# Forgetting attention with a SwiGLU block behind it: the stored order of batch 0's start is replaced

## The chip, the cores and the metric

The kernel runs on one core of a Trainium2 chip. The metric is the device time of one execution in microseconds, as a median over runs. Five engines work side by side and keep to their own order of instructions: TensorE (PE in the profile; its weight loads are PEld), VectorE (DVE), ScalarE (ACT), GpSimd (POOL) and SyncE (SP). SP, ACT and POOL also start DMA transfers.

## The reference

Everything is given and returned in float32; the kernel multiplies in bfloat16.

```
B, H, S, D = 8, 8, 576, 64
scores = q @ k.T / sqrt(D);  cum = cumsum(log(clip(f, 1e-4, 1)))
scores = where(causal, scores + cum[i] - cum[j], -1e9)
attn = softmax(scores) ;  x = attn @ v         # heads side by side: 4608 tokens x 512
xn = x / sqrt(mean(x*x) + 1e-6) * rms_g
out = (silu(xn @ w_gate) * (xn @ w_val)) @ w_out     # 512 -> 1536 -> 512
```

## The kernel before

The work is cut into some 1,550 pieces, each a few instructions of one engine. `ORDER`, a text of names, says in which order the pieces are emitted; every engine then runs its own pieces in that order, and a piece that must wait holds up all later pieces of its engine. Nothing else sets the order. `name@A`, `@D`, `@O` or `@S` puts a piece on ACT, DVE, POOL or SP in place of its default engine. `name*n` has `warm_up` (L249) issue idle matmuls on a tile of zeros, n blocks of 128 columns, in front of the piece; they compute nothing that is used, and only keep TensorE occupied.

The names that matter below, for batch b, pair of heads p, block of 128 tokens j:

- `Lq Lk Lv Lqk`: loads of q, k, v and of the tails (tokens 512 to 575) into ten staging buffers `st`. Batch 0 loads q and k in quarters of four heads by 256 tokens (`load_half`, L463); `Lq0.0` and `Lk0.0` are heads 0 to 3, tokens 0 to 255. `lf`: the load of f (L271, on ACT). `rg`: the 2 KB of rms_g (L352, on POOL). `wg0..2`, `wv0..2`, `wo0..1`: weights, cast on the way (L381, L393, on POOL).
- `Cq Ck Cqk`: the cast of a staged load to bf16 (L222). `Sv`: v times the decay (L451).
- `tr0.hp`: PE transposes of q and k of one pair (L540; `tr1.p`, `tr2.p` for batches 1 and 2, L528); `keeptr...q` and `.k`: their copies out of PSUM (L222). `trt`, `keeptrt`: the same for the tails (L558).
- `clip log scan expo twice turn_dec keep_dec`: the decay, from f to the factors that `Sv` needs. `fetch_ln`, `fetch`: the activation tables of Ln and Exp.
- `turn_rg keep_rgT spread_rg keep_rg`: rms_g turned and spread over the partitions (L357, L360, L366, L222).
- `far`: a mask written into the scores' PSUM bank (L664); `sc`: scores (L679); `esc`: their exp on ACT (L688); `msc`: a mask on POOL (L694). `sc4`, `exp4`, `mask4`: the tail's diagonal.
- `val`: probabilities times v (L714); `xpo`: the division, into X (L721, L722). `sq rs xn`: the norm (L729, L735, L739). `xtr kxtr`: the turned activations of batches 0 and 1 (L766, L222).
- `g v th ga hga`: gate and value products of a group of tokens, and the SwiGLU (L863, L868, L872, L879). `pj o so`: the last product, its copy and its store (L889, L222, L897). Groups 0 and 1 hold 256 tokens each, the others 512.

Batch 0 is worked in two parts: `HEAD`, tokens 0 to 255 (score banks named `.0`), so that group 0 can start early, and `REST` (banks `.512`, `.1024`, `.384`). The scores have two PSUM buffers (`sc`), the products of many kinds share three (`ff`), and one more (`po`) is for `val`. From `g0.0` on the attention of the next batches is laced between the products of the groups. TensorE's order before has 51 pieces ahead of `g0.0` and 64 from there to `g2.0`.

Of the kernel before, what the change touches and what calls it, by code (L numbers as in the profile page):

```python
# [14 lines left out]
B, H, S, D = 8, 8, 576, 64  # L15
# [7 lines left out]
one lf far Lq1.0 Lq0.0 Lq0.1@A ident Lk0.0 Lv0.1@A tri identb clear Lk0.1 Lq0.3@A fetch_ln rg Lk0.2 clip Lk0.3@A log Cq0.1@A scan Lq0.2 Cq0.0@A Lqk01  # L23
fetch Lv0.0 Ck0.0 tr0.01*72 Lqk11@A far0.1.0 keeptr0.01.q tr0.00 keeptr0.01.k far0.3.0 expo keeptr0.00.q sc0.1.0 Ck0.1@D Cq0.3@A twice keeptr0.00.k@D
tr0.02 Lv0.40 turn_dec esc0.1.0 Lk1.0 tr0.03 turn_rg Ck0.2@O Lqk00@A far0.0.0 keeptr0.03.q keep_rgT keeptr0.03.k sc0.0.0 Lqk10@A Ck0.3 sc0.3.0
keeptr0.02.k tr0.12 esc0.3.0 keep_dec Lq1.3 Cq0.2 keeptr0.02.q Sv0.1@O Lv0.2@A tr0.10*2 keeptr0.12.q far0.1.1024 esc0.0.0 keeptr0.12.k@D spread_rg
Cq1.0 Lv0.3 keeptr0.10.k Cqk0@D far0.2.0 keeptr0.10.q sc0.2.0 Lk1.3@A Sv0.0@O trt0 esc0.2.0 Lv0.41 keeptrt0 wv0 sc0.1.1024*6 Cqk1@A val0.0.0 Lk1.2
val0.4.0:ff keep_rg val0.6.0:ff xpo0.0.0 k4.0 Lk1.1 esc0.1.1024 val0.2.0:ff sc0.0.384 Lq1.2 wg0 xpo0.2.0 esc0.1.384 Lq1.1 sc4.0 xpo0.4.0 wg1 exp4.0
xpo0.6.0 esc0.3.384 far0.3.1024*4 esc0.0.384 Ck1.0 esc0.2.384 sc0.3.1024 Sv0.2 sq0.0 sc0.1.512 Lv1.41 trt1 esc0.3.1024 keeptrt1 Lv1.40 Sv0.3@O
esc0.1.512 Lqk20 sc0.0.512*9 Sv0.4 Lqk21 sq0.1 far0.0.1024*2 wv1 sc0.0.1024 esc0.0.512 rs0.0 Lk2.0 esc0.0.1024 sc0.2.512*6 tr1.0 mask4.0 xn0.1  # L30
far0.2.1024 keeptr1.0.q@A k4.1 Lv1.0 sc0.2.1024 esc0.2.512 keeptr1.0.k@D val0.0.2 val0.1.2:ff xpo0.0.2 esc0.2.1024 sc0.3.512 Cq1.2@O xpo0.1.2 val0.2.2
xn0.0 Ck1.1 esc0.3.512 val0.5.2:ff val0.3.2:ff xpo0.5.2 xtr0.0 wg2 sc1.0.512 Cq1.1@A kxtr0.0 xpo0.3.2 esc1.0.512 xtr0.1 Cq1.3 val0.4.2:ff xpo0.2.2
val0.6.2:ff wv2 Lq2.0 xpo0.4.2 kxtr0.1 val0.7.2 xpo0.6.2 Ck1.3@O tr1.1 esc1.0.0 xpo0.7.2 sc4.1 Ck1.2 g0.0 Lv1.3 keeptr1.1.k@D sq0.2 keeptr1.1.q v0.0f
th0.0 sq0.3 ga0.0 g0.2 exp4.1 sq0.4 hga0.0 sc1.0.1024 th0.2 rs0.2 tr1.3 esc1.1.512 ga0.2 xn0.2 v0.2f*4 keeptr1.3.q@A keeptr1.3.k@D esc1.0.1024 g0.4
hga0.2 xtr0.2 xn0.3 th0.4 tr1.2 kxtr0.2@A sc1.1.0 ga0.4 keeptr1.2.k xtr0.3 v0.4f esc1.1.1024 Lq2.3 kxtr0.3@D keeptr1.2.q g1.0 esc1.1.0 hga0.4 Lv1.1
v1.0f th1.0 msc1.1.1024 Lv1.2@A ga1.0 sc1.2.512 Lq3.3 esc1.2.512 g0.6 mask4.1 hga1.0 xn0.4 g1.2 Ck2.0 th0.6 ga0.6 v1.2f Sv1.4 th1.2 esc1.2.0 Lk2.1
ga1.2 g1.4 Cqk2@A hga1.2 xtr0.4 sc1.2.1024 th1.4 v0.6f kxtr0.4@A Lk2.3 Sv1.0@O ga1.4 esc1.2.1024 Lq2.1 g0.8 hga0.6 wo0 v1.4f th0.8 Cq2.0 esc1.3.512
ga0.8 v0.8f msc1.0.1024 Lqk31 hga1.4 g1.6 hga0.8 Lk3.0 msc1.2.1024 trt2 Sv1.2@D th1.6 sc1.3.0 keeptrt2@A wo1 v1.6f esc1.3.0 ga1.6 Lq3.2 Sv1.3 g1.8
hga1.6 Lqk30 tr2.0 th1.8 Sv1.1@D g0.10 keeptr2.0.k ga1.8 k4.2@A val1.4.0 keeptr2.0.q Cq2.3@A v1.8f th0.10 xpo1.4.0 val1.2.0:ff esc1.3.1024 ga0.10
val1.0.0 hga1.8 v0.10f Cq3.3@A msc1.3.1024 xpo1.0.0 Cq2.1@A tq3.3 g1.10 Ck2.1@A hga0.10 Ck2.3 xpo1.2.0 sc2.0.512 th1.10 val1.5.0 ga1.10 val1.3.0:ff  # L40
esc2.0.512 v1.10f xpo1.3.0 xpo1.5.0 val1.6.0:ff sc4.2 val1.1.0:ff xpo1.6.0 val1.7.0 xpo1.1.0 pj0.0.0 xpo1.7.0 hga1.10 sq1.1 sq1.0 tr2.1 exp4.2
pj0.0.0e sq1.3 keeptr2.1.q pj0.1.0 sq1.4 keeptr2.1.k@D Lk2.2 sq1.2 o0.0.0@D Lk3.3 Lq2.2@A rs1.0 pj0.1.0e esc2.0.0 pj1.0.0 Cqk3 xn1.1 Lv2.3@A tt3
o0.1.0 xn1.4 Lv2.0@A so0.1.0 pj1.0.0e Cq3.2@D sc2.0.1024 o1.0.0 xn1.2 xtr1.1 esc2.1.512 pj1.1.0 xn1.3 esc2.0.1024 xn1.0 kxtr1.1@D Lv2.1 Ck3.0@A
msc2.0.1024 xtr1.2 Ck2.2@A pj1.1.0e kxtr1.2 Lq3.0 tr2.3 o1.1.0 xtr1.3 tq3.2 Cq2.2 keeptr2.3.k sc2.1.0 kxtr1.3@D keeptr2.3.q@A Sv2.3 xtr1.0 tr2.2
Lv2.41@A kxtr1.0 Lk3.1 xtr1.4 keeptr2.2.q g2.0 keeptr2.2.k mask4.2 Lv2.40@A kxtr1.4 v2.0f Lq4.0 th2.0 esc2.1.1024 g2.1 ga2.0 Lq3.1 esc2.1.0 hga2.0
v2.1f tk3.0 g2.2 th2.1 Ck3.3@A ga2.1 sc2.2.512 th2.2 Sv2.4 hga2.1 v2.2f Lv2.2@A ga2.2 esc2.2.512 g2.3 hga2.2 Sv2.0 v2.3f th2.3 Lv6.40 Ck3.1@A ga2.3
msc2.1.1024 g2.4 Lv3.3 k4.3@A Lk3.2 hga2.3 esc2.2.0 v2.4f Sv2.1@D Lv3.40 g2.5 th2.4 Sv2.2 tk3.1 ga2.4 sc2.2.1024 th2.5 v2.5f esc2.2.1024 Lq4.1 ga2.5
hga2.4 Lk4.0 val2.0.0 esc2.3.512 msc2.2.1024 g2.6 hga2.5 tk3.3 Cq4.0@A Cq3.0@D v2.6f th2.6 Cq3.1@A ga2.6 sc2.3.0 Ck3.2@A tq3.1 xpo2.0.0 g2.7 esc2.3.0
hga2.6 v2.7f th2.7 tq3.0 esc2.3.1024 val2.4.0 ga2.7 val2.1.0:ff xpo2.4.0 g2.8 msc2.3.1024 Lv3.1 xpo2.1.0 val2.3.0 tk3.2 hga2.7 th2.8 Sv3.3 v2.8f ga2.8
val2.5.0:ff Lv3.41 xpo2.3.0 sc4.3 val2.7.0:ff Lqk41 xpo2.5.0 exp4.3 val2.2.0 mask4.3 so1.0.0@S hga2.8 sc3.0.512 xpo2.2.0 Lq4.3 esc3.0.512 g2.9 Sv3.1  # L50
xpo2.7.0 Lv3.2 val2.6.0 th2.9 Lv3.0 Ck4.0 v2.9f esc3.0.0 ga2.9 Sv3.4 Lk4.1 g2.10 xpo2.6.0 hga2.9 tk4.0 sc3.0.1024 th2.10 so0.0.0 v2.10f esc3.0.1024
ga2.10 g2.11 esc3.1.512 hga2.10 msc3.0.1024 v2.11f sq2.1 Sv3.2 th2.11 pj2.0.0 sq2.4 ga2.11 Lqk40 Cq4.1 sq2.2 Lk4.3 hga2.11 sq2.3 Lq4.2 sq2.0 pj2.0.0e
tq4.0 sc3.1.0 rs2.0 pj2.1.0 esc3.1.1024 esc3.1.0 xn2.0 xn2.4 tx2.0.3 msc3.1.1024 pj2.1.0e xn2.2 sc3.2.512 esc3.2.512 Lv4.2 pj2.2.0 Sv3.0 Lv4.3 o2.1.0
xn2.1 tx2.2.3 esc3.2.0 so2.1.0 o2.0.0 sc3.2.1024 so1.1.0 tx2.1.3 Cq4.2@A val3.0.0 Cq4.3@D esc3.2.1024 pj2.2.0e xpo3.0.0 pj2.3.0 tq4.3 esc3.3.512
msc3.2.1024 xn2.3 Ck4.3@D pj2.3.0e val3.1.0 Ck4.1@D tk4.3 o2.3.0 val3.3.0:ff xpo3.1.0 o2.2.0 val3.2.0:ff xpo3.3.0 sc3.3.0 tq4.1 xpo3.2.0 g3.0 Lk4.2
val3.5.0 th3.0 v3.0f Lv4.40 xpo3.5.0 esc3.3.0 Lv4.1 ga3.0 g3.1 esc3.3.1024 Cqk4@D Lk5.0 v3.1f hga3.0 th3.1 Lv4.41 msc3.3.1024 g3.2 ga3.1 tq4.2
val3.4.0 hga3.1 th3.2 val3.7.0:ff tk4.1 xpo3.4.0 v3.2f ga3.2 val3.6.0 xpo3.7.0 Lk6.2 g3.3 xpo3.6.0 Lq5.0 v3.3f hga3.2 tt4 th3.3 sq3.4 ga3.3 g3.4 sq3.2
hga3.3 v3.4f th3.4 Ck5.0@D sq3.1 ga3.4 g3.5 Lk5.1 Lq5.3 hga3.4 sc4.0.512 th3.5 Ck6.2 tk5.0 v3.5f Ck4.2@A ga3.5 Sv4.4 esc4.0.512 g3.6 hga3.5 tx2.3.4
# [907 lines left out]
```

## Time and profile before

| | |
|---|---|
| median of 5 runs | 381.34 us (380.26 to 382.61) |
| the profiled execution | 384.89 us, span 383.1 us |
| mean granted TensorE clock | 0.987 |
| PE busy | 367.3 us (96%) |
| DVE, ACT, POOL busy | 260.1, 220.4, 136.1 us |
| `g0.0`, first product of group 0, starts at | 37.29 us |
| `pj0.0.0`, first last-product, starts at | 69.11 us |
| `g2.0` starts at | 83.59 us |
| DMA moved | 52.58 MB |

Busy time is what an engine spent on instructions; an idle matmul counts as busy too. The row of the granted clock says how much of TensorE's full rate was granted in each slice. A row of a timeline gives start, length, engine, line, operation, and in brackets how long the engine stood idle ahead of it and what ended that. A DMA row gives the time from issue to landing. The times of `g0.0`, `pj0.0.0` and `g2.0` are read in PE's timeline, from the rows of L863 and L889 in their order.

### The profile page before, as it was taken

Reading aid. Unit: us, or ns where it says so; the run is one execution under the profiler, and the core shown is the slowest. Engines: PE = TensorE matmul, PEld = TensorE weight load, DVE = VectorE, ACT = ScalarE, POOL = GpSimd, SP = SyncE. Lnnn points to the kernel's source line nnn. Section 1 sums busy time; section 2 is a strip of 40 time slices with the busy share of each in tenths; the row PEclk is TensorE's granted clock in tenths of the full one; section 3 lists DMA queues with packets and bytes.
Section 4 is the critical chain, followed back from the end, with each engine's and each line's share of the span. In section 5 each row is a group of like instructions: output and inputs, shape, how many; then the busy total and the mean of one; then the engine's idle time right before and its main releaser. Section 6 shows DMA issues by size and latency. Waiting matters only on the chain.

```text
span 383.1 us, 8139 instructions
## 1 busy us (share of the span) xinstructions
PE 367.3 (96%) x3103; PEld 196.2 (51%) x3144; DVE 260.1 (68%) x497; ACT 220.4 (58%) x369; POOL 136.1 (36%) x249
## 2 busy tenths in 40 slices
PE   7779999999999999999899999999999999999996
PEld 3547788554644544445454544454445544444443
DVE  5547888678866778768757765778467876763560
ACT  5578978578697477354755587346565422322312
POOL 3556193236468145533431564020830111000001
PEclk9869999999999999999999999999999999999999
DMA  9999999597699889999959794641300234002002
GB/s 216 238 255 218 211 212 214 121 230 148 127 225 182 174 161 176 184 182 165 185 135 183 149 197 111 153 85 41 76 36 8 64 82 124 3 0 82 29 0 110
DMA packets 144774, 52.58 MB, mean 137 GB/s; under 512 B 128188, under 2 KB 141120, under 8 KB 144736
## 3 DMA queue, kind: packets, MB, share of 16 engines
q1 hardware_dynamic: 126992, 37.64, 50.8%
q0 software_dynamic: 6016, 8.79, 10.8%
q10 hardware_dynamic: 11728, 5.65, 6.1%
q8 instruction: 24, 0.39, 0.5%
q14 instruction: 14, 0.11, 0.1%
HBM read 37.90 MB, written 9.44 MB: 124 GB/s over the span
## 4 chain that ended last, share of the span: by engine, by line
PE 67%; DMA 10%; issue 6%; DVE 6%; ACT 5%; POOL 3%; SPq 1%; POOLq 0%; ACTq 0%; DVEq 0%
PE ff L863 41%; PE ff L889 16%; DMA st<-in_q_dram 5%; PE sc L679 4%; PE po L714 3%; DMA QK<-ld 3%; DVE xn L739 2%; ACT PT L688 2%; POOL PT L694 1%; ACT th L868 1%; DMA st<-in_k_dram 1%; DMA out_dram<-ores 1%; DVE X L722 1%; PE ff L714 1%; DVE hT L879 1%
## 5 line engine op out<-in xcount | busy, mean ns | idle before, releaser
L868 ACT ACTIVATE th<-ff 128x512 f32<-128x512 f32 x108 | 64.5, 597 | 91.4 <-PE ff L863 86.7
L863 PE MATMUL ff<-xT,wv 128*128 128x512 bf16 (+1 forms) x466 | 109.7, 357 | 1.1 <-DVE ga L872 0.4
L863 PE MATMUL ff<-xT,wg 128*128 128x512 bf16 (+1 forms) x464 | 109.3, 357 | 1.2 <-DVE X L722 0.2
L688 ACT ACTIVATE PT<-sc 128x1024 bf16<-128x1024 f32 (+2 forms) x100 | 96.2, 991 | 16.4 <-PE sc L679 14.3
L872 DVE SCALAR_TENSOR_TENSOR ga<-th,ff 128x512 f32<-128x512 f32 x108 | 74.0, 685 | 41.7 <-ACT th L868 41.2
L889 PE MATMUL ff<-wo,hT 128*128 128x512 bf16 (+1 forms) x433 | 97.4, 373 | 0.8 <-issue 0.2
L879 DVE SCALAR_TENSOR_TENSOR hT<-ga,ff 128x512 bf16<-128x512 f32 x108 | 73.7, 684 | 15.2 <-PE ff L863 6.5
L694 POOL TENSOR_SCALAR_AFFINE_SELECT PT<-PT 128x256 bf16<-128x256 bf16 (+1 forms) x84 | 43.1, 537 | 74.2 <-ACT PT L688 74.0
L863 PEld LDWEIGHTS <-wg 128*128 128x128 bf16 x480 | 45.2, 98 | 44.4 <-issue 2.1
L863 PEld LDWEIGHTS <-wv 128*128 128x128 bf16 x480 | 44.6, 98 | 43.5 <-issue 3.3
L889 PEld LDWEIGHTS <-hT 128*128 128x128 bf16 x444 | 42.4, 98 | 47.7 <-issue 1.4
L714 PEld LDWEIGHTS <-PT 128*128 128x128 bf16 x896 | 33.7, 98 | 11.8 <-issue 3.2
L739 DVE SCALAR_TENSOR_TENSOR xn<-X,rs,rgb 128x512 bf16<-128x512 f32 x40 | 32.8, 845 | 8.9 <-POOL rs L735 8.8
L897 POOL DMA_DIRECT2D out_dram<-ores x16 | 9.2, 578 | 68.2 <-ACT ores L222 36.0
L222 ACT COPY ores<-ff 128x512 f32<-128x512 f32 (+1 forms) x25 | 14.2, 569 | 33.2 <-PE ff L889 27.6
L222 POOL CAST ld<-st 128x512 bf16<-128x512 f32 x34 | 21.1, 628 | 30.6 <-DMA st<-in_q_dram 11.5
L679 PE MATMUL sc<-QK 64*128 64x256 bf16 (+3 forms) x272 | 29.0, 301 | 1.4 <-ACT QK L222 1.3
L735 POOL TENSOR_TENSOR rs<-sq,mhalf 128x5 f32<-128x5 f32 (+2 forms) x9 | 9.9, 1104 | 51.7 <-ACT junk L729 51.6
L729 ACT ACTIVATE junk<-X 128x513 bf16<-128x513 f32 x40 | 25.4, 635 | 3.9 <-DVE X L722 3.4
L451 POOL TENSOR_TENSOR Vs<-st,decT 128x512 bf16<-128x512 f32 x22 | 23.1, 1051 | 6.3 <-DMA st<-in_v_dram 5.9
L714 PE MATMUL po<-Vs,PT 128*128 128x65 bf16 x571 | 24.3, 194 | 0.1
L679 PEld LDWEIGHTS <-QK 64*128 64x128 bf16 x528 | 13.8, 96 | 20.0 <-issue 13.0
(90 smaller groups left out, 261.5 us busy)
## 6 DMA issues: line engine op xcount, KB each, us to landing
st<-in_k_dram SPq DMA_DIRECT2D x30, 256.0 KB, 4.5
st<-in_q_dram SPq DMA_DIRECT2D x29, 256.0 KB, 4.3
st<-in_v_dram SPq DMA_DIRECT2D x26, 256.0 KB, 4.3
out_dram<-ores POOLq DMA_DIRECT2D x15, 256.0 KB, 3.2
out_dram<-ores SPq DMA_DIRECT2D x12, 256.0 KB, 2.4
out_dram<-ores ACTq DMA_DIRECT2D x8, 256.0 KB, 2.7
st<-in_v_dram ACTq DMA_DIRECT2D x6, 256.0 KB, 4.6
wo<-in_moe_w_out_dram POOLq DMA_DIRECT2D x2, 768.0 KB, 9.3
```

The costliest lines, as they stand in the source:

```text
L222: {"DVE": nc.vector.tensor_copy, "POOL": nc.gpsimd.tensor_copy, "ACT": nc.scalar.copy}[eng](o, x)
L679: nc.tensor.matmul(sc[:, par, c:c + n], lhsT=k_cols(r, p, kj), rhs=q_cols(r, p, q0, n), start=not opened, stop=not opened or (kj, q0) == b ...
L688: nc.scalar.activation(T["pt", b, p][:, :, c0:c0 + n], T.pop(("sc", b, p, c0))[:, :, 0:n], ACT.Exp, scale=scale)
L694: nc.gpsimd.affine_select(out=d, in_=d, pattern=[[0, n], [1, 128]], compare_op=ALU.is_ge, fill=0.0, base=0, channel_multiplier=-1)
L714: nc.tensor.matmul(T["po", b, hs][:, qm, m, :], lhsT=w, rhs=Vs[i][:, kj, h, :], start=(kj == 0), stop=(kj == qi))
L729: nc.scalar.activation(junkp.tile([128, DM + 1], BF16, name="junk"), X[i][:, j, :], ACT.Square, scale=DM ** -0.5, accum_out=T["sq", b, js] ...
L739: nc.vector.scalar_tensor_tensor(xn, in0=X[i][:, j, 0:DM], scalar=T["rs", b, js][:, j:j + 1], in1=rgb, op0=ALU.mult, op1=ALU.mult)
L863: nc.tensor.matmul(ps[:, c * w:c * w + w], lhsT=wt[:, dc, (fc + c) * 128:(fc + c + 1) * 128], rhs=T["xT", g][:, dc, 0:w], start=(dc == 0), ...
L868: nc.scalar.activation(t, T["pg", g, fc], ACT.Tanh, scale=0.5)
L872: nc.vector.scalar_tensor_tensor(a, in0=T.pop(("th", g, fc)), scalar=1.0, in1=T.pop(("pg", g, fc)), op0=ALU.add, op1=ALU.mult)
L879: nc.vector.scalar_tensor_tensor(o, in0=T.pop(("ga", g, fc)).rearrange("p (c t) -> p c t", t=w), scalar=0.5, in1=T.pop(("pv", g, fc)).rear ...
L889: nc.tensor.matmul(po, lhsT=T["hT", g][:, fc, j * 128:(j + 1) * 128], rhs=wo[:, fc, c0:c1], start=(fc == 0), stop=(fc == NFC - 1))
```

## The change

Only `ORDER` is replaced; no function, buffer or size changes. The set of pieces is the same, and from `g2.0` on TensorE's own order is the same piece for piece. So are the sets of TensorE pieces ahead of `g0.0` (51), and from `g0.0` to `g2.0` (64); within them the order differs. In detail:

- The first loads are `Lq0.0` on ACT's queue and `Lk0.0` on SP's, in place of `lf` and of batch 1's `Lq1.0`. The tails of batch 0 follow, then the other loads of batch 0; batch 1's come behind them. `Lqk20`, `Lqk21` and `Lk2.0` move behind `g0.0`, and `wv2` too.
- On TensorE `tr0.01` and `tr0.00`, both turned from that first pair of loads, stand first, then `turn_rg` and `spread_rg`, then the scores.
- On POOL `rg` is issued ahead of `tri`. On DVE `keep_rgT` stands ahead of `keeptr0.01.q`, and `scan` behind `keeptr0.01.k`.
- Among other changes of engine, `Cqk1` moves from ACT to POOL, `keep_rg` from ACT to DVE, `k4.0` from POOL to DVE, `Sv0.0` from POOL to DVE.
- `xn0.0`, `xn0.1` and `xtr0.*` move ahead of most of `val0.*.2`.
- The idle matmuls shrink from 105 blocks to 67, and sit in other places.

The start of the diff, as far as `g0.0`; the rest are moves by a place or a few:

```diff
 ORDER = """
-one lf far Lq1.0 Lq0.0 Lq0.1@A ident Lk0.0 Lv0.1@A tri identb clear Lk0.1 Lq0.3@A fetch_ln rg Lk0.2 clip Lk0.3@A log Cq0.1@A scan Lq0.2 Cq0.0@A Lqk01
-fetch Lv0.0 Ck0.0 tr0.01*72 Lqk11@A far0.1.0 keeptr0.01.q tr0.00 keeptr0.01.k far0.3.0 expo keeptr0.00.q sc0.1.0 Ck0.1@D Cq0.3@A twice keeptr0.00.k@D
-tr0.02 Lv0.40 turn_dec esc0.1.0 Lk1.0 tr0.03 turn_rg Ck0.2@O Lqk00@A far0.0.0 keeptr0.03.q keep_rgT keeptr0.03.k sc0.0.0 Lqk10@A Ck0.3 sc0.3.0
-keeptr0.02.k tr0.12 esc0.3.0 keep_dec Lq1.3 Cq0.2 keeptr0.02.q Sv0.1@O Lv0.2@A tr0.10*2 keeptr0.12.q far0.1.1024 esc0.0.0 keeptr0.12.k@D spread_rg
-Cq1.0 Lv0.3 keeptr0.10.k Cqk0@D far0.2.0 keeptr0.10.q sc0.2.0 Lk1.3@A Sv0.0@O trt0 esc0.2.0 Lv0.41 keeptrt0 wv0 sc0.1.1024*6 Cqk1@A val0.0.0 Lk1.2
-val0.4.0:ff keep_rg val0.6.0:ff xpo0.0.0 k4.0 Lk1.1 esc0.1.1024 val0.2.0:ff sc0.0.384 Lq1.2 wg0 xpo0.2.0 esc0.1.384 Lq1.1 sc4.0 xpo0.4.0 wg1 exp4.0
-xpo0.6.0 esc0.3.384 far0.3.1024*4 esc0.0.384 Ck1.0 esc0.2.384 sc0.3.1024 Sv0.2 sq0.0 sc0.1.512 Lv1.41 trt1 esc0.3.1024 keeptrt1 Lv1.40 Sv0.3@O
-esc0.1.512 Lqk20 sc0.0.512*9 Sv0.4 Lqk21 sq0.1 far0.0.1024*2 wv1 sc0.0.1024 esc0.0.512 rs0.0 Lk2.0 esc0.0.1024 sc0.2.512*6 tr1.0 mask4.0 xn0.1
-far0.2.1024 keeptr1.0.q@A k4.1 Lv1.0 sc0.2.1024 esc0.2.512 keeptr1.0.k@D val0.0.2 val0.1.2:ff xpo0.0.2 esc0.2.1024 sc0.3.512 Cq1.2@O xpo0.1.2 val0.2.2
-xn0.0 Ck1.1 esc0.3.512 val0.5.2:ff val0.3.2:ff xpo0.5.2 xtr0.0 wg2 sc1.0.512 Cq1.1@A kxtr0.0 xpo0.3.2 esc1.0.512 xtr0.1 Cq1.3 val0.4.2:ff xpo0.2.2
-val0.6.2:ff wv2 Lq2.0 xpo0.4.2 kxtr0.1 val0.7.2 xpo0.6.2 Ck1.3@O tr1.1 esc1.0.0 xpo0.7.2 sc4.1 Ck1.2 g0.0 Lv1.3 keeptr1.1.k@D sq0.2 keeptr1.1.q v0.0f
...
+one Lq0.0@A far Lk0.0 Lqk01 lf ident Lq0.1@A Lqk00 rg identb clear Lq0.2@A Lk0.1 far0.1.0*16 fetch_ln Ck0.0@A Lk0.2 Cq0.0 Lv0.0 tr0.01*20 clip tr0.00
+log turn_rg Lv0.1 keep_rgT keeptr0.01.q keeptr0.00.k spread_rg keeptr0.01.k@D keeptr0.00.q@A Lk0.3@A scan far0.0.0 Lq0.3@A Cqk0 Cq0.1 fetch trt0*4
+Lv0.40 sc0.0.0 sc0.1.0 Ck0.1 keeptrt0 Lv0.3 Cq0.2@D esc0.0.0 keep_rg@D expo Ck0.2@O far0.3.0 tr0.03 tri esc0.1.0 tr0.10 twice Lv0.41 keeptr0.03.k
+turn_dec k4.0@D Lk1.0@A tr0.02 keep_dec sc4.0 Ck0.3@O keeptr0.03.q@A Lk1.1 Cq0.3@A Sv0.0 Lqk10 keeptr0.02.k@A tr0.12*8 keeptr0.10.k@D exp4.0 Lq1.0
+Lv0.2@A sc0.3.0 Sv0.1@O keeptr0.12.k@D Lqk11 esc0.3.0 keeptr0.10.q sc0.0.384*4 wg0 esc0.3.384 keeptr0.02.q far0.1.1024 esc0.0.384 sc0.1.1024
+esc0.1.384 wv0 esc0.2.384 val0.2.0 Lq1.1 val0.6.0:ff esc0.1.1024 far0.2.0 Lq1.3 xpo0.6.0 wg1 sc0.2.0 Lk1.3 keeptr0.12.q esc0.2.0 sc0.1.512 Sv0.4@O
+val0.0.0:ff xpo0.2.0 esc0.1.512 far0.3.1024 xpo0.0.0 val0.4.0 sc0.3.1024 Sv0.3 Ck1.1@A mask4.0 far0.2.1024 Lk1.2 esc0.3.1024 sc0.2.1024 xpo0.4.0
+Lv1.41 Sv0.2 sq0.1 Lq1.2 sq0.0 val0.3.2*8 Lv1.40 Cq1.0@D esc0.2.1024 val0.2.2:ff rs0.0 sc0.0.512 Ck1.0 esc0.0.512 xn0.0 far0.0.1024 sc0.0.1024 Lv1.1
+Cqk1 esc0.0.1024 sc0.2.512 xn0.1 wv1 trt1*2 tr1.0 esc0.2.512 xpo0.2.2 Cq1.1 keeptrt1 xtr0.1 keeptr1.0.q@A wg2 xpo0.3.2 xtr0.0 Lq2.0 keeptr1.0.k
+sc0.3.512 kxtr0.1@D val0.4.2 kxtr0.0 esc0.3.512 val0.5.2:ff k4.1@D val0.1.2:ff Cq1.3@A tr1.1 xpo0.1.2 Lv1.0 sc1.0.512 keeptr1.1.k xpo0.5.2 val0.0.2:ff
+esc1.0.512 xpo0.4.2 val0.7.2:ff xpo0.0.2 val0.6.2 keeptr1.1.q@A xpo0.7.2 sc4.1 g0.0 esc1.0.0 xpo0.6.2 Ck1.3 v0.0f th0.0 sq0.3 g0.2 ga0.0 sq0.4 Ck1.2
...
```

## The prediction

> **What bounds the kernel now.** I read the page's first parts, then the busy time by stages, then ACT's timeline and the waits of the first 37 us, and last the DMA rows. The page:
>
> ```profile
> span 383.1 us, 8139 instructions
> PE 367.3 (96%) x3103; PEld 196.2 (51%) x3144; DVE 260.1 (68%) x497; ACT 220.4 (58%) x369; POOL 136.1 (36%) x249
> ...
> PEclk9869999999999999999999999999999999999999
> DMA  9999999597699889999959794641300234002002
> ```
>
> TensorE is the bound over the whole, but 96% counts idle matmuls. The clock falls well below full in the second and third slices alone (9.6 us each). DMA is full up to slice seven, 67 us, and has a hole from 67 to 77. By stages (busy time of each engine, granted clock, DMA share, GB/s):
>
> ```profile
> 5.46:8.87 3.41, 2.64 (x19) 1.24 (x18) 1.86 (x4) 2.80 (x5) 0.60 (x1) 1.00 1.22 266
> 8.87:12.29 3.42, 2.13 (x28) 1.39 (x25) 1.59 (x5) 2.05 (x5) 0.20 (x1) 1.00 1.22 287
> 12.29:15.70 3.41, 3.25 (x29) 2.53 (x29) 2.68 (x8) 1.42 (x3) 2.02 (x4) 0.50 1.36 195
> 15.70:19.11 3.41, 2.12 (x26) 1.61 (x24) 1.79 (x5) 1.79 (x3) 2.66 (x6) 1.00 1.22 242
> 19.11:22.53 3.42, 1.73 (x48) 1.40 (x48) 1.30 (x6) 1.86 (x3) 2.83 (x5) 1.00 1.31 232
> 22.53:25.94 3.41, 2.72 (x24) 1.50 (x24) 2.11 (x7) 2.79 (x9) 1.93 (x3) 0.50 1.25 287
> 25.94:29.36 3.42, 3.27 (x25) 1.44 (x23) 1.91 (x6) 3.03 (x5) 1.32 (x2) 0.50 1.22 237
> 37.29:69.11 31.82, 31.43 (x426) 26.14 (x424) 26.62 (x50) 25.80 (x44) 15.04 (x27) 1.00 1.11 212
> ```
>
> From g0.0 (37.29) on TensorE is busy 31.43 of 31.82 us with real products: nothing to win there except by starting earlier. Ahead of it TensorE waits or idles, and runs 10.2 us at half clock. What releases the batch-0 part is ACT, which needs every exp of it:
>
> ```profile
> 14.62 0.81 ACT L688 ACTIVATE PT<-sc 128x768 bf16<-128x768 f32 x1 [1.99 <-PE sc L679]
> 17.74 0.81 ACT L688 ACTIVATE PT<-sc 128x768 bf16<-128x768 f32 x1 [1.06 <-POOL Vs L452]
> 20.67 0.62 ACT L222 CAST ld<-st 128x512 bf16<-128x512 f32 x1 [2.12 <-DMA st<-in_q_dram]
> 21.19 0.58 ACT L222 COPY rgb<-ff 128x512 f32<-128x512 f32 x1
> 31.39 2.86 ACT L688 ACTIVATE PT<-sc 128x1024 bf16<-128x1024 f32 x3
> ```
>
> The first exp is at 11.83, the last of batch 0 ends at 34.25. In those 22.42 us ACT is busy 15.71 (busy time of that window). The cast at 20.67 is Cqk1, batch 1's tails, standing in front of batch 0's exps until its load lands; the copy behind it is keep_rg, for whose bank TensorE waits 1.2 us. Last, two DMA rows (KB, us from issue to landing), the second being wo1, issued at 56.76:
>
> ```profile
> rg<-in_moe_rms_g_dram POOLq DMA_DIRECT2D x1, 2.0 KB, 6.6
> wo<-in_moe_w_out_dram POOLq DMA_DIRECT2D x1, 768.0 KB, 10.2
> ```
>
> **The change part by part.** The end shifts by what g0.0 and then g2.0 shift, since TensorE's order behind g2.0 is unchanged and the DMA hole of 67 to 77 cuts any backlog: behind it every load is started by an event that shifts along.
>
> *To the first exp: nothing gained, 11.9.* Lq0.0 and Lk0.0 now go first, on two queues; the first two loads before took 3.0 and 4.0 us, so both are there at 0.82 + 3.7 = 4.5. The cast takes 0.60 (POOL row), the eight transposes 0.56: done at 5.7, where the old order had its first pair turned at 8.6. But turn_rg is the next TensorE piece, and keep_rgT stands on DVE ahead of keeptr0.01.q. rg is issued 1.1 us sooner than 3.17, without tri ahead of it, and by its row lands at 2.1 + 6.6 = 8.7. From there: turn_rg 0.26, keep_rgT 0.15, spread_rg 0.60, far0.0.0 0.49, the idle matmul and trt0 0.61, sc0.0.0 0.34, handovers 0.1: 11.25. TensorE stands still from 5.7 to 8.7; windows of 3.41 us with 1.73 or 2.13 us busy were followed by half clock (table), so 8.87 to 12.29 is at half, and far took 0.80 for 0.49 there: I add 0.3 for far and 0.35 for the rest. First exp at 11.9.
>
> Here the Trainium skill speaks otherwise ("DMA: Bandwidth & Descriptors", section "Anatomy of one DMA — SWDGE (gpsimd) path"): such a DMA has a fixed cost near 2.0 us. That would land rg at 4.2, ahead of the transposes; the first exp would then wait for ACT's own queue (f issued at 1.43, landing 3.8 later, clip 0.45, Ln 0.68, two copies 0.64, two issues 1.0, table and warm-up 1.48) and start at 10.4, a gain of 1.4. This case's row, 6.6 for the same transfer in the same stretch, decides; it cannot land much sooner than the 3.8 of f.
>
> *ACT from first to last exp: 2.9 gained.* Its new queue holds, by start-to-start times of the timeline: 4 HEAD exps at 0.71, expo 0.68, 2 small copies at 0.32, casts Cq0.3 and Ck1.1 at 0.52, exp4 0.28, 4 exps of 256 columns at 0.26, 8 of 1,024 at 0.95, 2 squares at 0.72, 2 copies at 0.48: 16.5. Two DMA issues (Lk1.0, Lv0.2) 0.5. Waits before were 22.42 − 15.71 = 6.7; of them 2.12 (Cqk1), 1.06 and 1.99 lose their cause, 1.5 stays, and I add 0.8 for sc0.3.0, which stands behind tr0.12 and so behind the landing of q0.3 (3.03 MB ahead of it and with it, at 270 GB/s from 2.1: 13.3; cast, transposes, score: 15.5, when ACT is at 15.4 anyway). The last exp ends at 11.9 + 16.5 + 0.5 + 2.3 = 31.2, before 34.25.
>
> *From the last exp to g0.0: 1.1 gained.* Before, 3.04 us: DVE ran without a gap from 32.1 to 37.6 through eight divisions, xn0.0 (1.21) and a transposed copy. xn0.0, xn0.1 and their copies now come ahead; behind the last exp stand two val of 0.38, sc4.1 and divisions at 0.48: 2.0. g0.0 at 33.2, 4.1 earlier. What moved to DVE and POOL (keep_rg 0.58, Sv0.0 0.94, k4.0, Cqk1 0.60) lies in gaps: DVE is busy 21.8 of 37.3 us, POOL 20.3; without that cover it would cost its 2.4 us.
>
> *From g0.0 to pj0.0.0: about 1.1 given back.* Same TensorE pieces, but DMA carried this stretch at 1.11 of a full 1.22. The loads named ahead of wo1 in the two orders add up to the same 17.4 MB (sizes from the shapes, weights in float32), so wo1 can come forward only by filling the slack, (1.22 − 1.11)/1.22 x 31.8 = 2.9 us at most, and at least by nothing; I take half, 1.4: landing at 65.6 for 67.0. Before, pj0.0.0 started 2.1 us after it. So pj0.0.0 is at best 3.5 earlier. wv2 is such a case too (landed 46.85; its product started at 52.5, 5.7 of slack against 4.1): hidden. Batch 2's tails and Lk2.0, moved behind g0.0, are wanted at 57 and 59.5, when before they had landed by 40 to 42: hidden. The shift left is 3.5 at best; half a microsecond off for the late weights' uneven landing: 3.0.
>
> *Idle matmuls.* 67 blocks for 105. Those of the start ran beside waiting; the ones behind 22 us, at half clock, took about 3 us on TensorE but lay beside ACT's queue. Zero, inside the terms above. The clock is worth more: 6.8 us at half from 22.53 to 29.36 slow TensorE's part of the ACT chain. By the row they vanish (included above as lost waits). The skill ("TensorE: Matmul & The Clock Gate", Part 1, "What's actually happening") says that the activity window is free-running and does not start with the kernel. An order searched against one phase then keeps its full clock only in some executions: by that rule the two half-clock stretches return at other places, for another 0 to 1.5 us lost. The profile shows one phase only (changes at 12.29, 15.70, 22.53, 29.36); I put this into the range.
>
> Sum on the profiled execution: 384.89 (span 383.05 and 1.84 around it) − 3.0 = 381.9. The median of runs stands 3.55 below that execution; the shift carried over gives 381.34 − 3.0 = **378.3**.
>
> **The rivals.** A measurement of this kernel can tell about 0.5%, 1.9 us.
>
> *DMA keeps the gain.* wo1 lands at 66.5 to 67.5 and the stall at pj0.0.0 lets the clock fall; for it speaks that DMA is full in the first 67 us, against it the 1.11 share and the 2.1 us behind the landing. Gain 0 to 2: 380.3.
>
> *More than forecast.* rg lands by 6 us, the clock stays full, and wo1, issued earlier on POOL, uses all 2.9 us of slack: first exp 10.4, g0.0 at 31.7, pj0.0.0 up to 5.0 earlier: 376.2.
>
> *Slower.* keep_rgT waits for rg at the head of DVE's queue, with both first copies, scan and thus expo, keep_dec and all Sv behind it. If rg, the only software transfer among batch-0 loads on full engines, lands late, each microsecond goes onto the first exp and half clock onto what follows. It decides from 8.7 + 3.0 = 11.7 on; at 13.5 all is 1.8 plus about 0.7 of clock late: 383.8. Against it: 6.6 was measured beside full queues as well.
>
> *That it doesn't do what it says:* the pair is turned first, yet its exp is no earlier; this is in my main case, the gain coming from ACT's queue. A clock no better than before is in the range.
>
> **How the numbers follow.** Main case (gain 2 to 4.4) 0.52; DMA keeps it (0 to 2) 0.21; more (4.4 to 6.5) 0.19; slower 0.08, 0.06 of it by over 1.9. Faster by over 0.5%: 0.52 + 0.19 = 0.71; within: 0.21 + 0.02 = 0.23; slower 0.06. The range leaves out the slow case and the far end of the gains: 375.4 to 381.4.
>
> **What would show it.** Right: a wait of TensorE of 2 to 3 us ahead of L357 released by rg's DMA; a first exp near 12; no ACT wait over 1.5 us behind it; the last batch-0 exp near 31, g0.0 near 33, pj0.0.0 near 66, g2.0 near 80.6; from there equal. Wrong: a first exp at 10 or at 14; g0.0 early but g2.0 not (DMA); half clock between 16 and 33 for over 4 us; or a stretch behind 83 us that differs by over a microsecond.

## The result and the profile after

The changed kernel takes **380.38 us** (median of 44 runs, 378.91 to 383.57), the kernel before, on the same chip, 382.52 us (79 runs, 380.26 to 385.42). The ratio is **0.9955, 95% interval 0.9942 to 0.9967**: 1.7 us gained by it, between 1.3 and 2.2; the two medians lie 2.1 us apart. The forecast was a shift of 3.0 us, to 378.3. So the sign was right, and most times up to g2.0 came near the forecast, but the size of the gain in the medians did not. The profiled execution after took 380.12 us. Its page (span, busy time of TensorE and the other engines, granted clock and DMA share in 40 slices):

```profile
span 378.2 us, 8114 instructions
PE 364.8 (96%) x3095; PEld 195.5 (52%) x3136; DVE 259.8 (69%) x500; ACT 219.9 (58%) x368; POOL 135.9 (36%) x247
...
PEclk9599999999999999999999999999999999999999
DMA  8999999996989999998949693641300234002003
```

Half clock now shows in the second slice and no longer in the third. By stages (busy time of PE, PEld, DVE, ACT and POOL, granted clock, DMA share, GB/s):

```profile
5.03:8.44 3.41, 1.63 (x14) 0.95 (x13) 1.03 (x4) 1.33 (x4) 0.60 (x1) 1.00 1.18 240
8.44:11.86 3.42, 2.87 (x20) 1.57 (x19) 2.84 (x7) 1.85 (x3) 2.34 (x4) 0.50 1.26 264
11.86:15.27 3.41, 2.92 (x23) 2.47 (x23) 1.91 (x6) 2.17 (x4) 1.95 (x6) 0.50 1.30 242
15.27:18.68 3.41, 3.41 (x31) 1.80 (x31) 3.38 (x6) 1.76 (x4) 2.91 (x4) 0.50 1.17 260
18.68:22.10 3.42, 3.15 (x60) 2.06 (x57) 2.52 (x8) 3.29 (x8) 3.26 (x7) 1.00 1.26 229
...
33.86:66.93 33.07, 31.99 (x433) 26.83 (x433) 26.62 (x55) 26.78 (x44) 16.43 (x30) 1.00 1.14 215
```

TensorE is at half clock from 8.44 to 18.68: three windows of 3.41 us, 10.2 us in all, as long as in the profile before, only earlier. ACT's timeline from the first exp to the last of batch 0 (start, length; in brackets the idle time ahead and what ended it):

```profile
11.49 0.81 ACT L688 ACTIVATE PT<-sc 128x768 bf16<-128x768 f32 x1 [0.67 <-PE sc L679]
...
15.85 0.62 ACT L222 CAST ld<-st 128x512 bf16<-128x512 f32 x1 [1.41 <-DMA st<-in_q_dram]
...
18.09 0.81 ACT L688 ACTIVATE PT<-sc 128x768 bf16<-128x768 f32 x1 [1.06 <-PE sc L679]
...
30.20 1.07 ACT L688 ACTIVATE PT<-sc 128x1024 bf16<-128x1024 f32 x1
```

The cast of batch 1's tails, and the 2.12 us that ACT stood in front of it, are gone from this row; no wait from the first exp to the last of batch 0 is over 1.5 us. TensorE's row for rg:

```profile
7.60 0.22 PE L357 MATMUL ff<-ident_f,rg 4*128 4x4 f32 x1 [1.27 <-DMA rg<-in_moe_rms_g_dram]
```

And the two DMA rows of the forecast (KB, us from issue to landing), the second being wo1, issued at 56.50:

```profile
rg<-in_moe_rms_g_dram POOLq DMA_DIRECT2D x1, 2.0 KB, 5.5
...
wo<-in_moe_w_out_dram POOLq DMA_DIRECT2D x1, 768.0 KB, 9.7
```

Against the profile before: g0.0 at 33.86 (before 37.29), pj0.0.0 at 66.93 (69.11), g2.0 at 80.71 (83.59). From g2.0 to the span's end it is 297.5 us (before 299.5), although TensorE, DVE, ACT and POOL each have the same instructions in the same order there. The longest wait of TensorE between g0.0 and pj0.0.0, 0.72 us, is for DVE:

```profile
38.47 0.34 PE L253 MATMUL ff<-idle 128*128 128x128 bf16 x3 [0.72 <-DVE hT L879]
```

### The profile page after: what moved, and what is told of

Same layout as the page of the kernel before. It is cut to its first block, busy times and chain, and to the rows that moved or that the text cites. A ratio compares the mean times of both kernels' runs of the same rounds, so it can differ in the third digit from the quotient of the medians.

```text
span 378.2 us, 8114 instructions
## 1 busy us (share of the span) xinstructions
PE 364.8 (96%) x3095; PEld 195.5 (52%) x3136; DVE 259.8 (69%) x500; ACT 219.9 (58%) x368; POOL 135.9 (36%) x247
## 3 DMA queue, kind: packets, MB, share of 16 engines
q0 software_dynamic: 6016, 8.79, 10.5%
## 4 chain that ended last, share of the span: by engine, by line
PE 83%; POOL 4%; issue 3%; DMA 3%; ACT 3%; DVE 2%; SPq 0%; POOLq 0%; ACTq 0%
PE ff L863 48%; PE ff L889 21%; PE sc L679 5%; PE po L714 4%; PE ff L714 2%; DMA st<-in_q_dram 2%; DMA out_dram<-ores 1%; POOL Vs L451 1%; ACT PT L688 1%; PE ff L528 1%; POOL rs L735 1%; DVE xn L739 1%; POOL PT L694 1%; PE ff L766 1%; ACT th L868 1%
## 5 line engine op out<-in xcount | busy, mean ns | idle before, releaser
L222 POOL CAST ld<-st 128x512 bf16<-128x512 f32 x32 | 21.1, 670 | 23.3 <-DMA st<-in_q_dram 12.0
```

The costliest lines, as they stand in the source:

```text
L222: {"DVE": nc.vector.tensor_copy, "POOL": nc.gpsimd.tensor_copy, "ACT": nc.scalar.copy}[eng](o, x)
```

## The experiments

Each ratio compares a kernel with runs of the kernel before on the same chip. The times of g0.0 and g2.0 come from one profiled execution of each kernel. The questions: why a shift of 2.9 us at g2.0 in the profiles is 1.7 to 2 us in the medians; where the gain arises; and what the wait for rg, the clock and the idle matmuls are worth.

### Both kernels once more, and two halves

`before_again` and `after_again` are unchanged. `head_g0` has the changed order up to `g0.0` and then the remaining names in the old order; `before_g0` the reverse.

> The kernel before, unchanged, for a second profile. Theory A (the change acts ahead of g2.0 alone, and what the first pair of profiles shows behind it is chance of one execution): g2.0 at 83 to 84 us, and from g2.0 to the end about 297.5 us as in the profile after, not the 299.5 of the first profile before; the 0.95 us wait of L679 for a DMA at 183.7 us is gone. Theory B (the old order's loads come late in the middle every time): 299.5 us again, with that wait. Ratio 1.000 by both.

> The changed kernel, unchanged, for a second profile. Theory A: ratio 0.9955, g0.0 at 33.9, g2.0 at 80.7 us, 297.5 us behind it. Rival C (the head itself differs from run to run, by where the half clock falls): turn_rg still near 7.6, but half clock over other stretches than 8.4 to 18.7 us, and g2.0 away from 80.7 by a microsecond or more.

> The changed order as far as g0.0, the old order for all behind it. Theory H (the gain arises ahead of g0.0 alone): ratio 0.9955, g0.0 at 33.9, g2.0 near 81. Rival S (between g0.0 and g2.0 the old order of loads and copies gives the gain back, so that the new order of that stretch is needed): g0.0 at 33.9, but g2.0 at 82.5 or later, ratio 0.998 or more.

> The old order as far as g0.0, the changed order for all behind it. Theory H: g0.0 at 37.3, g2.0 at 83.6, ratio 1.000. Rival S: g0.0 at 37.3, but g2.0 at 82.5 or earlier, ratio 0.998 or less.

| kernel | median | ratio (95%) | g0.0 | g2.0 | g2.0 to end |
|---|---|---|---|---|---|
| before_again | 382.74 | 1.0009 (0.9986 to 1.0031) | 37.70 | 84.00 | 298.1 |
| after_again | 380.27 | 0.9941 (0.9925 to 0.9957) | 33.85 | 80.71 | 297.2 |
| head_g0 | 382.27 | 1.0000 (0.9975 to 1.0026) | 33.95 | 82.14 | 297.4 |
| before_g0 | 383.16 | 1.0012 (0.9996 to 1.0029) | 35.99 | 82.96 | 298.0 |

The 299.5 us of the first profile before were mostly chance: of the 2 us over after's 297.5, 0.95 is one wait of TensorE for a late load, gone in before_again:

```profile
183.72 0.23 PE L679 MATMUL sc<-QT,QK 64*128 64x64 bf16 x4 [0.95 <-DMA QK<-ld]
```

From g0.0 to g2.0 the old order takes 46.30 and 46.30 us in these two profiles of before, and the new order 46.85 and 46.86 in those of after: this stretch hardly varies from one execution to the next. The new body (all behind g0.0) with the old head gains nothing in the medians. But the new head with the old body gains nothing either, and only both together do. By POOL's and DVE's timelines of head_g0:

```profile
48.81 0.61 POOL L222 CAST ld<-st 128x512 bf16<-128x512 f32 x1 [2.94 <-DMA st<-in_k_dram]
...
53.66 2.65 POOL L694 TENSOR_SCALAR_AFFINE_SELECT PT<-PT 128x256 bf16<-128x256 bf16 x6
56.27 0.84 POOL L393 DMA_DIRECT2D wo<-in_moe_w_out_dram  x1
```

```profile
53.89 3.28 DVE L451 TENSOR_TENSOR Vs<-st,decT 128x512 bf16<-128x512 f32 x1
...
58.54 0.69 DVE L451 TENSOR_TENSOR Vs<-st,decT 128x512 bf16<-128x512 f32 x1
```

The first row is Ck2.0. The changed head leaves its load, Lk2.0, behind g0.0, and in the old body the cast stands on POOL ahead of the multiplications Sv1 and of wo0 and wo1; the changed body has it on ACT. POOL waits 2.94 us, its later work runs as one unbroken row, and beside that row a multiplication on DVE takes 3.28 us in place of 0.69. It ends at 57.17, and 0.69 us before that, at 56.48, POOL's selects had ended (56.31) and only the issue of wo1 ran. The Trainium skill ("SBUF — State Buffer", "Who interferes with whom") says that a DVE instruction with two inputs in SBUF and a GpSimd instruction that reads SBUF exclude each other for a whole instruction. The rows fit that, but here the DVE instruction lasts through several instructions of POOL, not one; that it waited all that time is argued from the lengths.

### What takes the head's gain

`head_g0_sv` puts one of the two DVE multiplications on POOL, `head_g0_sv2` both; `head_g0_ck` leaves them and moves the cast. Against head_g0, cut to the pieces that differ:

```diff
 head_g0_sv:   -Sv1.2@D  +Sv1.2
 head_g0_sv2:  -Sv1.2@D  +Sv1.2   -Sv1.1@D  +Sv1.1
 head_g0_ck:   -g1.2 Ck2.0 th0.6     +g1.2 th0.6
               -wo1 v1.6f            +wo1 Ck2.0 v1.6f
```

> As head_g0 (the changed order as far as g0.0, the old one behind), with Sv1.2 on POOL in place of DVE. In head_g0 that one multiplication took 3.28 us on DVE, where others of its shape take 0.69, beside an unbroken row of POOL instructions from 53.1 to 57.1, and L528 waited 1.22 us behind it. Theory P (the head gives its gain with the old body too, and this collision alone took it): g2.0 near 80.9, no DVE row of L451 over 1.1 us ahead of 62, ratio 0.995. Rival S (the old body gives the gain back in other places too): g2.0 at 81.7 or later, ratio 0.998 to 1.000.

> As head_g0, with both multiplications of batch 1 that stood on DVE (Sv1.2, Sv1.1) on POOL, as the changed order has them. In head_g0 and head_g0_sv one of them took 3.28 and 3.49 us on DVE beside an unbroken row of POOL. Theory P (this collision is what takes the head's gain in the old body): no such row, g2.0 at 80.7 to 81.5, ratio 0.994 to 0.996. Rival S (the old body gives the gain back at other places as well, or POOL with two more multiplications becomes late for wo1): g2.0 at 82 or later, ratio 0.998 or more.

> As head_g0, with one piece moved: Ck2.0, POOL's cast of k of batch 2, from ahead of the Sv1 multiplications to behind the issue of wo1. In head_g0 POOL stood 2.94 us for that load (4.5 and 5.0 in head_g0_sv and head_g0_sv2), because the changed head puts Lk2.0 behind g0.0, and all of POOL's row behind it came late. Theory K (this one wait takes the head's gain in the old body): POOL has no wait for in_k ahead of wo0, no multiplication of over 1.2 us on DVE, g2.0 at 80 to 81.5, ratio 0.993 to 0.996. Rival S (the late v loads, or the order of products and copies in the old body, take it as well): g2.0 at 82 or later, ratio 0.998 or more.

head_g0_sv: 385.86 us, ratio 1.0102 (1.0076 to 1.0127). head_g0_sv2: 385.51, ratio 1.0073 (1.0049 to 1.0096). Both misses: POOL waited 4.48 and 5.00 us for the same load, and then had more to do behind it. In the first the collision came again, and TensorE stood 3.77 us:

```profile
55.61 3.49 DVE L451 TENSOR_TENSOR Vs<-st,decT 128x512 bf16<-128x512 f32 x1
...
58.15 0.88 POOL L393 DMA_DIRECT2D wo<-in_moe_w_out_dram  x1
```

Again the last 0.69 us of the multiplication (from 58.41) lie beside the issue of wo1. In the second there was no collision, and TensorE stood 4.11 us for POOL itself. So the collision is a follow-up, not the cause. **head_g0_ck: 380.32 us, ratio 0.9940 (0.9922 to 0.9958)**: one cast moved, and by the medians the old body keeps all of the gain. POOL's wait for in_k is gone from its timeline (what is left is 0.87 for v), and no multiplication on DVE ahead of 62 us is over 1.04. But the profiles do not show where the gain comes: g2.0 was expected at 81.5 at the latest and came at 82.28, against head_g0's 82.14, and both profiled executions took 381.22 us. For head_g0 that is 1.05 below its median, for head_g0_ck 0.9 above. That moving the cast gives the gain back is shown by the medians; the path inside the kernel is not shown.

So the gain arises ahead of g0.0; what the new body adds, by the medians, is that a load moved behind g0.0 holds nothing up.

### One wait of ACT

`before_cqk1` takes two pieces out of ACT's row in the old order, and nothing else:

```diff
-Cqk1@A
+Cqk1
-keep_rg
+keep_rg@D
```

> The kernel before with two pieces taken from ACT: Cqk1 (on POOL) and keep_rg (on DVE). The step on record: ACT's wait of 2.1 us for Cqk1's load and two casts of 0.6 leave ACT's row, and g0.0 comes 1 to 2.5 us earlier, near 35.5; ratio 0.995 if that carries on, 1.000 if the stretch up to g2.0 gives it back as in head_g0. Rival (ACT only waits elsewhere, for the loads of q0.2 and q1.x that the old order puts late): g0.0 within 0.5 us of 37.3, ratio 1.000.

381.29 us, ratio 0.9983 (0.9964 to 1.0002): 0.7 us, just not told from nothing. Its profiled execution had g0.0 at 33.97 and g2.0 at 80.28, as early as the changed kernel's. The ACT wait of the forecast is in the traces, but in the medians its removal, together with keep_rg, is worth about a third of the gain (0 to 1.4 us by its interval). ACT's row shows one reason: behind the fourth exp, where the cast used to stand, the next exp now waits 1.65 us for its scores.

```profile
19.14 1.02 ACT L688 ACTIVATE PT<-sc 128x1024 bf16<-128x1024 f32 x1 [1.65 <-PE sc L679]
```

### Further profiles of both kernels

> The kernel before once more, for its profile. Two profiles of it so far (run times 384.89 and 383.80) had three windows of 3.41 us at half clock, as a quarter of its executions; two of three executions have two windows and a time of 382.1. Theory W: with two windows g2.0 lies near 82.3, with three near 83.8. Rival: g2.0 near 83.6 whatever the windows, and the time differs behind g2.0.

> The kernel before, a fourth profile. Theory W2 (the wait of ACT for batch 1's tails, Cqk1, has another length in each execution: 2.1, 2.5 and 1.0 us so far, with g0.0 at 37.3, 37.7 and 35.3): a wait of 1.0 to 2.6, and g0.0 and the time follow it, 35.3 and 381.2 at the short end, 37.7 and 383.8 or more at the long end. Rival: g0.0 does not follow that wait.

> The changed kernel, a third profile. Theory W2: with Cqk1 out of ACT's row the head has one length: g0.0 within 0.3 us of 33.86, time 379.5 to 380.8. Rival: g0.0 spreads by a microsecond or more here too.

The same row, ACT's cast of batch 1's tails, in the four executions of before, in the order of the table:

```profile
20.67 0.62 ACT L222 CAST ld<-st 128x512 bf16<-128x512 f32 x1 [2.12 <-DMA st<-in_q_dram]
```

```profile
21.02 0.62 ACT L222 CAST ld<-st 128x512 bf16<-128x512 f32 x1 [2.46 <-DMA st<-in_q_dram]
```

```profile
19.25 0.62 ACT L222 CAST ld<-st 128x512 bf16<-128x512 f32 x1 [1.02 <-DMA st<-in_q_dram]
```

```profile
20.71 0.62 ACT L222 CAST ld<-st 128x512 bf16<-128x512 f32 x1 [2.19 <-DMA st<-in_q_dram]
```

| execution | time | wait for Cqk1 | half clock ahead of g0.0 | g0.0 | g2.0 | g2.0 to end |
|---|---|---|---|---|---|---|
| before, first | 384.89 | 2.12 | 10.2 | 37.29 | 83.59 | 299.5 |
| before_again | 383.80 | 2.46 | 10.2 | 37.70 | 84.00 | 298.1 |
| before_look | 381.17 | 1.02 | 6.8 | 35.25 | 81.57 | 297.9 |
| before_look2 | 383.38 | 2.19 | 10.2 | 37.33 | 83.64 | 298.0 |
| after, first | 380.12 | none | 10.2 | 33.86 | 80.71 | 297.5 |
| after_again | 379.79 | none | 6.8 | 33.85 | 80.71 | 297.2 |
| after_look | 379.10 | none | 3.4 | 32.78 | 79.65 | 297.6 |

In these four g0.0 follows the wait, over 2 us between executions of one kernel; though that is one short execution against three long ones. Why the load lands later in one execution than in another stays open. From g0.0 to g2.0 all four take 46.30 to 46.32 us, so that what differs ahead of g2.0 differs ahead of g0.0. Of the 2.04 us by which before_look is earlier at g0.0 than the first profile, 0.34 lie ahead of the first exp, 1.1 are the shorter wait for Cqk1 (the other ACT waits of over 0.15 us from the first exp up to there add up to 3.05 and 3.04), and 0.6 lie behind that cast. The forecast read its 2.12 from a long execution. The expectation that the changed head has one length was wrong too: g0.0 spreads over 1.1 us in the three profiles of after.

The runs without a shown profile fit. Every run comes with its mean granted clock, and each window of 3.41 us at half clock takes 0.0045 off it. Of 229 runs of before (two more had next to no half clock), 153 had a clock of 0.989 to 0.992 (two windows) and a mean of 382.1 us, 62 had 0.985 to 0.988 (three) and 383.4, eight had one window and 380.9, six had four and 384.2. The first profile, with 0.987, was of the second kind. Of 66 runs of after the means with one, two and three windows are 380.0, 381.0 and 380.7.

### The clock and the idle matmuls

```diff
 before_warm: +far0.1.0*8 sc0.1.0*8 tr0.12*4 trt0*18 sc0.2.0*4 val0.2.0*5
 after_warm:  +turn_rg*8 spread_rg*3 far0.3.0*6 sc0.0.512*8   -trt0*4 +trt0*14
 nofill:      every *n of the changed order left out
```

> The kernel before with 47 more blocks of idle matmuls ahead of g0.0 (36 to 55 more places where TensorE was seen to stand for a load or a copy), nothing else. Theory W (before runs with half clock over 6.8 us in most executions and over 10.2 us in some, the profiled ones among them, and the latter are 1.3 us longer; that is why a shift read from its profile is more than its median loses): the half-clock stretches ahead of g0.0 shrink to one window of 3.4 us or none, and the median falls to about 381.3, ratio 0.997. Rival D (those 1.3 us come from late loads, which let both the clock and the time go): the clock rises and the time stays, ratio 1.000.

> The changed kernel with idle matmuls also in the four holes of TensorE's first 13 us (turn_rg*8, spread_rg*3, trt0*14, far0.3.0*6) and sc0.0.512*8. Theory W: half clock over 3.4 us or not at all, in place of 6.8 to 10.2, and up to 1 us saved: the executions of the changed kernel with one half-clock window had 379.9, those with none 378.9. Ratio 0.991 to 0.993. Rival: ACT and the loads set the head, so that TensorE's clock there is free: ratio 0.995, first exp still near 11.5 and g0.0 near 33.9.

> The changed kernel without any of its 67 blocks of idle matmuls. Theory W: half clock over 14 us or more of the first 34, first exp 0.3 to 0.6 later, g0.0 near 35, ratio 0.998 to 1.000. Rival (the head is set by ACT and loads): more half clock but g0.0 within 0.3 us of 33.9, ratio 0.995.

before_warm: 381.96 us, ratio 0.9986 (0.9964 to 1.0007), with 1.3 half-clock windows per run on average in place of 2.3. after_warm: 380.18 us, ratio 0.9938 (0.9919 to 0.9958), full clock in the profile from the first record on, g0.0 at 33.49. By its medians before_warm gains 0.3 to 0.5 us for one window fewer (its interval reaches from a loss of 0.3 to a gain of 1.4), where runs of the old order that differ by one window of their own differ by 1.3. This speaks for late loads behind most of that 1.3, which make TensorE stand, and for the clock as a companion; the interval does not settle it. The profiled execution of before_warm fits: two windows of half clock, and still g0.0 at 37.22, with a long wait for Cqk1:

```profile
20.90 0.62 ACT L222 CAST ld<-st 128x512 bf16<-128x512 f32 x1 [2.60 <-DMA st<-in_q_dram]
```

nofill: 381.16 us, ratio 0.9976 (0.9961 to 0.9992), about 0.8 us more than the changed kernel's 380.3, and g0.0 at 34.82. About so much the idle matmuls are worth, though its interval overlaps that of the changed kernel's first runs by a little. Here the page shows a full clock everywhere, and is wrong about it. A window of nofill, and eight transposes of the same shape early and late:

```profile
11.83:15.24 3.41, 3.00 (x24) 2.56 (x24) 1.85 (x6) 2.08 (x4) 1.84 (x6) 1.00 1.30 245
```

```profile
16.37 1.03 PE L540 MATMUL ff<-ident,ld 128*128 128x128 bf16 x8 [0.58 <-ACT ld L222]
```

```profile
29.26 0.61 PE L528 MATMUL ff<-ident,ld 128*128 128x128 bf16 x8
```

Eight take 1.03 us at 16.4 and 0.61 at 29.3: early on about 0.6 of the later rate. A mask of four matmuls takes 0.82 us at 2.5, 0.83 at 20.8 and 0.50 at 24.0. The first clock record of this execution is at 23.3, and what lies ahead of it is printed as 1.00. Ahead of the first record the duration of a matmul tells the clock, not the row. So the mean clock of a run, too, can be printed too high: 17 of nofill's 22 runs have 0.999 or more.

### The wait for rg, and an earlier first exp

```diff
 rg_late: turn_rg from ahead of Lv0.1 to behind sc0.1.0; keep_rgT, spread_rg to behind keeptrt0
 early:   rg_late, and trt0*4 from ahead of sc0.0.0 to behind turn_rg; fetch to ahead of Lq0.3@A
```

> The changed kernel with turn_rg, keep_rgT and spread_rg behind sc0.1.0 in place of ahead of the first copies. The step on record (the wait for rg's 2 KB holds the first exp): TensorE no longer stands ahead of L357, DVE copies the first pair from 6.9 instead of 8.0, and the first exp starts near 10.5 instead of 11.5, g0.0 0.5 to 1 us earlier, ratio 0.992. Rival T (the first exp waits for trt0 in front of sc0.0.0, that is for the tails of q and k, which land at 9.2, and for ACT's second table, loaded at 9.3): the first exp stays within 0.3 of 11.5 and g0.0 at 33.9, ratio 0.995.

> As rg_late, and besides trt0 behind turn_rg, so that neither score of the first exp stands behind the tails' landing, and fetch (the Exp table) ahead of the issue of Lq0.3. Theory: in rg_late the first exp came at 10.73 because TensorE stood 3.1 us for the tails in front of sc0.0.0; without it the first exp starts when the table is there, at 9.0 to 9.5, but g0.0 gains less than half of that (0 to 0.6 over rg_late's 33.38), since ACT then meets the landing of q0.3 at 15 us. Ratio 0.992 to 0.994. Rival (first exp decides): g0.0 at 32.2, ratio 0.990.

rg_late: 380.53 us, ratio 0.9953 (0.9930 to 0.9975); first exp at 10.73, g0.0 at 33.38. The first exp came near the 10.5 expected of the forecast's step, but the ratio did not move: TensorE stood elsewhere, for the tails, as the rival had it:

```profile
9.97 0.40 PE L558 MATMUL ff<-ident,ld 128*128 128x128 bf16 x4 [3.05 <-POOL ld L222]
```

early: 379.71 us, ratio 0.9932 (0.9915 to 0.9949); first exp at 9.27, 2.2 us sooner than in after, and g0.0 at 33.49, 0.4 sooner, which is less than the spread of g0.0 in after (32.78 to 33.86). ACT gives the difference back, most of it at 13.87:

```profile
13.87 0.37 ACT L222 COPY QK<-ff 128x256 bf16<-128x256 bf16 x1 [2.46 <-DVE QK L222]
14.54 0.62 ACT L222 CAST ld<-st 128x512 bf16<-128x512 f32 x1 [0.30 <-DMA st<-in_q_dram]
```

The first exp doesn't decide. What does is not taken apart: here ACT waits 2.46 us for a copy of DVE, whose transposes stand on TensorE behind trt0 (10.18), spread_rg (11.25) and a mask (12.10), and for the landing of q0.3 only 0.30; in the next kernel the wait for q0.3 is 2.69. `early_warm` adds 33 blocks of idle matmuls to early (its expectation counted 29):

```diff
-tr0.01*20 sc0.0.0 trt0*4 spread_rg sc0.0.384*4
+tr0.01*26 sc0.0.0*6 trt0*14 spread_rg*5 sc0.0.384*10
```

> As early, with 29 more blocks of idle matmuls in the holes of TensorE ahead of 18 us. Theory (half clock in the head costs little, as after_warm showed): half-clock stretches vanish, g0.0 0.1 to 0.4 earlier than 33.49, ratio 0.992 to 0.993. Rival (the clock is what the new head still lacks): ratio 0.990 or less.

379.87 us, ratio 0.9953 (0.9931 to 0.9975), full clock from the first record on, g0.0 at 33.12: no better. early has the lowest ratio of all, but its interval overlaps those of the changed kernel (0.9955 and 0.9941), so it beats before and isn't shown to beat after.

## Why the prediction was right or wrong, point by point

- **First exp at 11.9, nothing gained: right** (11.49, and 11.83 before). The wait for rg was sized too long: it landed 5.5 us after its issue, not 6.6, and TensorE stood 1.27 us ahead of turn_rg, not 2 to 3. To go by the trace and not by the 2.0 us of the Trainium skill ("DMA: Bandwidth & Descriptors", "Anatomy of one DMA — SWDGE (gpsimd) path") was right. The terms of its other case, ACT's own queue, add up to 9.5, not 10.4; in the trace the Exp table and its warm-up were done at 10.8, since ACT also stood 1.55 us around the issue of Lq0.3. So rg held the exp by 0.8 us only: with it out of the way (rg_late) the tails and the table were next in line.
- **ACT from first to last exp, 19.3 us, last end at 31.2: right.** From 11.49 to 31.27 it is 19.8; the waits were 0.42, 1.41 and 1.06 and some small ones, where 2.3 was put in. (By its own terms the gain of this step is 3.1, not 2.9.) q0.3 came late: its cast started as it landed, at 15.85, where 13.3 was worked out.
- **g0.0 at 33.2: 33.86**; the 2.0 us behind the last exp were 2.6. A gain of 3.4, not 4.1.
- **1.1 given back up to g2.0: 0.55, and not to DMA** (from g0.0 to g2.0 46.85 us, before 46.30). The forecast gave it to late weights, but from g0.0 to pj0.0.0 TensorE has no wait over 0.15 us for a load. It stood 1.08 us for DVE (0.39 before), 0.72 of it at 38.47. wo1 landed at 66.2 against 65.6 forecast, pj0.0.0 came at 66.93 against "66 or later". "Batch 2's tails and Lk2.0, moved behind g0.0, are hidden" holds for the changed order, with Ck2.0 on ACT; head_g0's median shows the price where it stands on POOL, all of the gain.
- **g2.0 at 80.6, shift 3.0: 80.71, shift 2.88.** The sum over the steps came out right against the profile that it was made from, in part by luck: 0.7 us less gained at g0.0, 0.55 less given back.
- **"From there equal": true of the instructions, not of that pair of executions.** "A stretch behind 83 us that differs by over a microsecond" was named as a sign of being wrong, and it came: 299.5 against 297.5. The other profiles of before (297.9 to 298.1) take 1.5 of it back as chance; 0.6 us against the 297.4 of after remains, unexplained.
- **The clock:** "half clock between 16 and 33 for over 4 us" did not come (2.7 us). "By the row they vanish" was wrong: they moved to the front. The clock "is worth more" than the idle matmuls, the forecast said: taking half clock away was worth about 0.4 us in the old order (before_warm) and 0.2 in the new (after_warm), neither told from nothing. Nor does the busy time of a window tell the clock of the next: 1.73 and 2.13 us were followed by half clock, as the prediction says, but 2.12 (15.70 to 19.11, in the same table) by full clock.
- **The step that failed is the last one: "the shift carried over gives 381.34 − 3.0".** It took the 3.55 us by which the profiled execution stood above its median as common to both kernels. They are not: about 1.5 of them lay behind g2.0 by chance, and about 2 lay in the very stretch that the change rewrites, since before_look, near the median that was given, has g0.0 at 35.25 and a Cqk1 wait of 1.02 in place of 2.12. Against before_look the changed kernel's g2.0 is only 0.9 us earlier, against the first profile 2.9. The term mis-sized is the 2.12 of Cqk1, with the 0.9 us that lie ahead of the first exp and behind that cast. And the base: the five runs gave 381.34, the 79 beside the changed kernel 382.52. So of the 2.0 us between 378.3 and 380.38, 1.2 are the base and 0.9 the shift (3.0 against the 2.1 between the medians).
- **The rivals.** "DMA keeps the gain" gave the right time (380.3) by luck: the stall at pj0.0.0 that it named isn't there. "Slower by rg" did not come near its point of 11.7.

What stays open: the mean of g2.0 over four profiles of before and three of after differs by 2.8 us, the medians of all runs by 1.7 to 2.3. The profiled executions of before lie 1.0 us above the median of its runs on average, those of after 0.7 below. With so few, that can be chance. And which parts of the new head make up the other two thirds of the gain beside Cqk1 and keep_rg was not taken apart; nor is it seen in a profile how the moved cast of head_g0_ck brings the gain back.

## What to carry to other kernels

A wait for a load that a profile shows has the length of that execution. Before its removal is booked in full, ask how far the profile stands from the median, take a second profile, and see whether the excess lies in the stretch that the change rewrites. When a load is moved later, look for the instruction that first waits for it and for what is queued behind that one on its engine: here one cast at its old place cost, by the medians, as much as the whole change gained. And halves of an order spliced together measure their own seams: mend the seam before drawing the conclusion.

## What the runs showed of the hardware that was not expected

- A two-input multiplication on DVE of 0.69 us took 3.28 and 3.49 us beside an unbroken row of POOL instructions: it lasted through several of them, and ended 0.9 us after the last of them, about as the DMA issue that followed did.
- The granted clock is printed as full ahead of an execution's first clock record, while matmuls of known shape ran slower (eight transposes 1.03 against 0.61 us, a mask 0.82 against 0.50), in nofill from 2.5 to about 23 us.
- The same program with the same order had g0.0 between 35.25 and 37.70 us, while from g0.0 to g2.0 it took 46.30 to 46.32 us. From g2.0 to the end it took 297.9 to 299.5; nofill, with the same instructions there, took 296.6.
- A transfer of 2 KB by POOL's queue among full DMA engines took 6.5 to 6.8 us in the four profiles of before and 5.4 to 5.6 in the three of after.
